# Two first loads without a cast on the hardware queues, and a new written-out order, in an attention and mixer kernel

## The chip, the cores and the metric

One core of one Trainium2 chip. The metric is the time of one launch on the device in microseconds (us). The kernel before has a median of 415.73 us in 3 runs (415.58 to 415.92). One execution was profiled; its trace gives every instruction and every transfer.

Engines: PE (TensorE, matrix products), DVE (VectorE), ACT (ScalarE), POOL (GpSimd) and SP (SyncE). POOL, SP and ACT issue transfers (DMA). Transfers that POOL issues can cast float32 to bfloat16 on the way; this kernel issues all its casting loads there. What SP and ACT issue is not cast.

## The reference: what is computed

Linformer attention, then one mixer block, all inputs float32. B = 8 batches, H = 8 heads, S = 1024 positions, D = 64.

```python
k_proj = np.einsum('ks,bhsd->bhkd', E, k)        # 64 rows in place of 1024
v_proj = np.einsum('ks,bhsd->bhkd', F, v)
scores = scale * np.matmul(q, k_proj.transpose(0, 1, 3, 2))
...
attn = attn / (np.sum(attn, axis=-1, keepdims=True) + 1e-09)
x = np.matmul(attn, v_proj)                      # heads side by side: (8, 1024, 512)
...
h = np.maximum(x.transpose(0, 2, 1) @ w_tok1, 0.0) @ w_tok2
u = x + h.transpose(0, 2, 1)
h2 = np.maximum(u @ w_ch1, 0.0) @ w_ch2
return u + h2
```

## The kernel before

**Work.** For each batch: kv_proj (L503) projects k and v with E and F, two heads at a time in batch 0; k_transpose (L564) and q_transpose_pe (L608) turn k and q on PE; scores (L630) multiplies them, and ACT takes the exponential; attend (L658) multiplies with v, where a column of ones gives the sum of each row; DVE takes its reciprocal into rdn (L686) and multiplies (L692) into x. The token mixing follows (L1050 and L1079 in batch 0, others later), then the channel mixing: up_set (L1163, matmuls in L1180) and down_block (L1254, matmuls in L1289), each as a Strassen-like scheme of seven products. Nearly all of PE's time goes to the channel mixing.

**Batch 0.** Everything stands still until its data are there. The heads come in pairs; the pair of heads 2 and 3 is worked first, then 4 and 5, 0 and 1, 6 and 7. A pair's k, v and q are three loads of 512 KB each in memory (256 KB once they are bfloat16). All come by POOL's queue: 12 loads for the attention of batch 0, then w_tok1 (two), w_tok2, w_ch1 (six), w_ch2 (four), with batch 1 between and behind them. E and F come as float32 on SP's and ACT's queues (L257, L258) into the tile o0, which only later holds outputs; PE turns them (L462) with an identity matrix that POOL makes (L450), and ACT and DVE copy them to EFT as bfloat16 (L465).

**What sets the order.** The function adds jobs to a Planner (L116): each has an engine, a time that the author gives it, what it reads and writes, and a function that issues the instructions. plan() (L158) does not choose: it decodes ORDER, a string with two characters for each job, and SPOTS, one digit for each use of a PSUM bank. The jobs are issued in that order, and each engine executes its own in the order issued. FILLS names the places in the order ahead of which PE gets a product of zeros (blank, L435) that nobody reads. So ORDER, SPOTS and FILLS are the schedule of all engines, POOL's loads included; the times in the jobs served whoever made the strings and do not reach the chip.

At the start PE executes four products of zeros (L446), two of bfloat16 and two of float32. HWK (L90) is 0: the lines at 260 and 379 that would load k and v uncast do nothing.

**Reciprocals.** rdn_t (L295) has two tiles; attention pair g writes tile g % 2, so the next but one pair writes over it.

Of the kernel before, what the change touches and what calls it, by code (L numbers as in the profile page):

```python
# [9 lines left out]
F32 = mybir.dt.float32  # L10
# [10 lines left out]
    "4w3o5A424x4y0l5B4e0j4h5p4b4f454j464i4k3r5C4z0m43475D5E4l444-0o4m503s4o4n3t4+4p5q525t514B5F4q5r4C495s"
    "530p544D3Z5y3u5w0q5H3bA15x4J3c3a6B5u5I554K5z4r4G4L5K5v4A4H9v5L9x6D484I5+6E0r6F564M6C5-6G6O4N6A606P6Q"
    "626H6I6L4O636561646Z6J674s666K4EA26a57684F6M6b696N4Q0n6f4P6U6g6R6W4R6S6h6Y4U4S6V6c6i6T6X5S4T6d6j6k6u"
    "6l6e5T6m6n6x6+6v5U6o4V6-6y6z716p5a6q4W5G705b725J746r7A73756s765M6t776wA35N7B5O585Q787C5R4t5X5P795Y7J"
    "7F7K7D7G7H7Q7EA57I5Z7L7R5dA759A85eA65VA95fAAA45W5c5h5g5i7V7S5l7TAD7Z7X4X5m5j7a7n5k5n7b7o7W7d5o9z7M7e"
    "7p9-7c7O7q7g7P7r7h7N7f7sAF7i7uAH7Y7lAG7t7m7v7jAJ837wAIANAK7x84ALAOAhAM7z7yAiAP877kAj857U7+88AQAb8986"
    "ARAS8AAcAdAk8BAWAlAm8L9yAZ8CAYAeAT8DAfAaAg8FAUAXAV8M8G8EENB3At7-Az8N8mAEA+8+8i8n8TA-EO8k8oAuAvABAn8H"
    "8U8pB4B5AC8-8q81B0Aq8r92Ao8J90Ap938QArAs8jB6AwB18tB2B795Ax8uB88R8l91Ay8s96B9948v8w9G978x8yBB9H988SBD"
    "999I8KBE9KBCBF8z8WBGEP8VEQ9L9ABABI9N9BBJBH9O9+8X9JBKBNA0BLBO8Y9QBM829MBPBRBSBV8I8aBWBQBTBk9R80BYBXBl"
    "8bBZBUBn9PBc8OBdBa9SBeBfBpBbBh8PBgBmBiER9CBj8ZBo9YEVES9TBr9ZEUBqET8eBs9aEW8f8c9UBu8d9g9W9E9hEYBtC1Bz"  # L30
    "9dEZC2B-9iBwC59VC3BxC69eC48gC89D8hEbC9Bv9bEdC0Ec9c9FEfEj9fCBEeEgEkElCC9jB+EmEhEi9kEn9XEpEr9lC7EoCFCA"
    "By9nCGEsEtCDEq9oCEEu9mCJCHEvEwExCI9r9pCKCXEyEz9qCLCYCME+CNCZEaE-F09sCaILCOCPF19tIMCbDACREXCcF2F4F3Cd"
    "CQ9uF5CeF6CpCfF7FBDCChCSFCDEF9CqDFFADSCiCgFDCrDICTFEDGDJF8FGCjFHFFDHFLDTFICxCkFMFJFPClDUCmFKDLDBDVFQ"
    "FNDDDMFTCVCyINFUFRFODKCnFWDWFXCuDXDNFYCvCzFaCwFVDZFbDQDaC+DRFiFcDODcFSDPFZFdFfFeIPFjFgDdCUFhFlIRDYIT"
    "DkDbISCsIQCWDlFkIUIOC-CoFmFnDeD0CtFoFpDoFqD2DpD1D3FxIXDmD4D6DnIWFzFsFrDrD5FtDqDsFuF-DtD7G0DfDuD8G1Dv"
    "DwF+G2DgG3E0FvG4E1DiDxFwIZE2DyG6IbD+E8G7DjE9IcDzIdGDEAIaE5FyGEG9DhIeGAE6IfD-IhIgGHIiGFIjGIG5GGIkG8IY"
    "GVInE7GKMKIoGBImEBGCGLIsIlECItIuIpGNIqIrIvGOE3IwEDGWE4IxI-GZJ0EEIyGaEFJ1EGIzI+EJEHGXJ5EIJ2GYGcJ3J4GJ"
# [12 lines left out]
    "PiRRPgRcOOPhRSOvRMRTRPRUOwUJRdRVPjRWPaRXUNRfUKRZRYOyULRaRhUMPlRgRbReUOPmPwRiPkRjPnPxRkOzPcPoOmO+PpRl"  # L50
    "RmPyO-PqRnOnRrRoQ2RtOxRvPrQ3RwRpP0Q4RqP1RxP2S7RyPsRzPuUPPbR+P-UQRuPvURS0RsQ0S8S1UUSBUVQ1S9SCS3UWSAQ5"
    "PdUTUXS4SEUYUZUSR-SDSFS2UaSGQ6UbUdS5Q7SJUePtUfUcQ9UgUhSPT3SHSKSQUoQASIUpS6STT2UrUqSUSRT6UsSSQBSWUlUt"
    "QCSXPzUmT7T4P+UnUiQ8TASZUjUkShSLT8UxUuT9QDUvSaUwSVUzQESYU-SiU+V0TBSbT5QFV1TCSNV2QGTDSjUyV4P3TETcScV5"
    "V3TFSpV6SqSdSOV9SfV7VASeTGTdVDSMTKV8THTeSrTIVHTJVBVISmVETLVFVCSnVKTgVLVMThTMSoVJTfVOVGTjTNVPVWTkTOVQ"
    "TiTPVRTlVTSsVNStVUVXTRVSTmTSSgVZVVTQTnVaTuTTToSuSkTpTWTqSwTXSxTYVdVYSySlTsSzTvVeTUSvVbVlTVVgVpVnS+Vf"
    "VqVcS-TwVmVtT0U0VuVoT1W1VhU1W2TaViVwVjVrVxU2W5VkWJW6VvWKTzVyT+WNT-V-W8W0VzU3WOW9W7VsU4WAV+WQTrWPTZWR"
    "WLWSW3WDU5W4X0TtWBWyWTTbWCXIWMWzWVW+WUTxWEX1TyWFU7U6U8WWX4W-U9UBWXWbUAWZX2XaX3UCX5WcXbUDXJX7WYXcWdWH"
    "X6XdWGXMX8WgXNX9WhXPXCXQXAXDXeWiWjXfWaXOXBXEXKXGWmXRXLWIWkXUWlWnXVXhWoWeXiXWXgWqXjWrXmWfXnXkXoXSWsXs"
    "XTWpWtXtXlXHUEXYWuXZXuXpWvXqXFX-XXX+WwXxWxXyXvY9XzXrY0XwY1Y4Y2Y3Y6Y5Y7YAYDY8YBYCYJYFYEYMYGYKYNYHYLYO"
    "YIYPYQ"  # L60
)
SPOTS = (
    "3024101126436327273643040127120236363170420436171063240217145624732113405063774765765024721257605205"
    "6726211311072323401724223063354705252601467407364317023117417326261333177136413604752570156153207422"
    "0717501237102275300221337643164504125123103737627351104724633607633666334154626574653573657273116524"
    "1713476526117451111000431363504562017414020567306256407306640427552552201753173152014723475602015723"
    "0720475332734202200176315612415716323744645200150524671"
)
FILLS = (21, 21, 21, 21, 21, 21, 21, 27, 27, 30, 36, 36, 36, 36, 49, 62, 62, 66, 66, 79, 79)
# [20 lines left out]
HWK = 0  # L90
# [97 lines left out]
def kernel(  # L188
# [54 lines left out]
    def tile_of(shape, dtype, name):  # L243
        return sb.tile(shape, dtype, tag=name, name=name)
# [15 lines left out]
    for i, queue in enumerate((nc.sync, nc.scalar)[:HWK]):  # L260
        queue.dma_start(out=kv32[i], in_=(k, v)[i][0, 0:2].rearrange("h (p si) d -> p h si d", p=P))
# [33 lines left out]
    rdn_t = [tile_of([P, NJ, 2, 2], F32, f"rdn{i}") for i in range(2)]  # L295
# [82 lines left out]
    lead = (1.95, 2.45, 3.2)[HWK]  # L378
    for i in range(HWK):
        pl.add("SPQ", 1.6 + 1.1 * HWK, 1.6 + 1.1 * HWK, lambda: None, writes=[("kv32", i)], prio=-1001)  # L380
        if i:
            act(
                1024, lambda: nc.scalar.copy(out=v_sb[:, 0:2], in_=kv32[1]),
                reads=[("kv32", i)], writes=[("v", 0), ("v", 1)], prio=-100,
            )
        else:
            dve(
                1024, lambda: nc.vector.tensor_copy(out=k_sb[:, 0:2], in_=kv32[0]),
                reads=[("kv32", i)], writes=[("k", 0), ("k", 1)], prio=-100,
            )  # L390
# [63 lines left out]
    opening.append(pl.add("POOL", 1.0, 3.2, identities, writes=["ident"], prio=-150))  # L454
    pl.opening = opening

    for n in range(2):
        b = Bank("S", full=False)

        def turn(n=n, b=b):  # L460
# [9 lines left out]
        pl.add("PE", 0.9, 0.9, turn, reads=["ident"], takes=[b], prio=-150).mms = NJ  # L470
# [1091 lines left out]
```

## Time and profile before

| what | value |
| --- | --- |
| median of 3 runs | 415.73 us |
| the profiled execution: its time | 415.69 us |
| the profiled execution: first to last instruction (span) | 413.9 us |
| granted TensorE clock | 0.999 |
| DVE, ACT, POOL busy | 86%, 54%, 16% of the span |
| casting loads on POOL's queue: share of 16 engines | 55.7% of the span |
| E and F: issue to landing | 3.2 and 3.8 us |
| PE waiting, all waits that the profile lists | 3.4 us, 2.3 of it for the first loads of q and for the first memset |

The time of a run is the span and what lies around it, 1.8 us here. A busy PE is one with any matmul under way; a row of the timeline lasts from the first start to the last end, and matmuls overlap, so the pace is read from the starts. In the answers on windows, the columns are the stretch and its length, busy us and count of instructions for PE, its weight loads (PEld), DVE, ACT and POOL, then the granted clock, the mean busy share of the DMA engines and the GB/s that were written. Of a casting load, the written bytes are half of the read ones.

### The profile page before, as it was taken

The numbers are of one execution on the slowest core, as the hardware profiler recorded it, in microseconds if no ns is written. First come the engines' busy times: TensorE is split into PE (matmuls) and PEld (weight loads), VectorE is DVE, ScalarE is ACT, GpSimd is POOL, SyncE is SP. The second block draws the span as 40 slices with busy tenths as digits, with TensorE's granted clock in tenths as the row PEclk, the third lists the DMA queues.
The fourth block names the chain that finished last, engine by engine and source line by source line (L and its number), as shares of the span: only waits on it lengthen the run. The fifth ranks groups of instructions, "written<-read, shape, count | busy, mean of one in ns | idle before, by whom it ended". The sixth has DMA issues, their size and how long they took to land.

```text
span 413.9 us, 9589 instructions
## 1 busy us (share of the span) xinstructions
PE 406.4 (98%) x3909; PEld 344.4 (83%) x3911; DVE 355.9 (86%) x773; ACT 221.9 (54%) x429; POOL 66.8 (16%) x105
## 2 busy tenths in 40 slices
PE   8899999999999999999999999999999999999996
PEld 4489888688888888979988899888988798998896
DVE  2289899779999999989979798898989899988686
ACT  1647884258635664574754646455644745445520
POOL 8544021021102120112001112012100001010010
PEclk9999999999999999999999999999999999999999
DMA  8999999997998897978966869873996212251115
GB/s 153 205 202 204 207 190 192 160 172 170 189 166 168 201 170 143 166 156 156 245 118 127 133 148 178 143 167 89 180 227 118 52 51 103 52 115 39 52 69 187
DMA packets 93755, 61.69 MB, mean 149 GB/s; under 512 B 59024, under 2 KB 89232, under 8 KB 93712
## 3 DMA queue, kind: packets, MB, share of 16 engines
q0 software_dynamic: 35088, 45.09, 55.7%
q1 hardware_dynamic: 58256, 15.47, 22.8%
q8 instruction: 30, 0.49, 0.5%
q10 hardware_dynamic: 368, 0.52, 0.3%
q14 instruction: 13, 0.11, 0.1%
HBM read 59.24 MB, written 16.78 MB: 184 GB/s over the span
## 4 chain that ended last, share of the span: by engine, by line
PE 92%; DMA 4%; DVE 2%; POOL 1%; issue 1%; POOLq 0%; DVEq 0%
PE psum L1289 36%; PE psum L1180 35%; PE psum L991 5%; PE psum L875 4%; PE psum L672 3%; PE psum L521 3%; DMA q_sb<-in_q_dram 3%; PE psum L637 2%; DMA v_sb<-in_v_dram 1%; PE psum L712 1%; PE psum L1060 1%; PE psum L736 1%; DVE u L1105 1%; PE psum L1092 1%; PE psum L618 1%
## 5 line engine op out<-in xcount | busy, mean ns | idle before, releaser
L1289 PEld LDWEIGHTS <-G 128*128 128x128 bf16 x1356 | 130.0, 98 | 18.3 <-issue 3.5
L1289 PE MATMUL psum<-wc_sb,G 128*128 128x256 bf16 (+1 forms) x780 | 101.5, 271 | 0.0
L1180 PEld LDWEIGHTS <-wc_sb 128*128 128x128 bf16 x768 | 73.9, 98 | 10.5 <-issue 2.1
L1202 ACT ACTIVATE G<-psum 128x512 bf16<-128x512 f32 x96 | 56.2, 601 | 44.8 <-PE psum L1180 44.3
L1289 PE MATMUL psum<-wT,G 128*128 128x256 bf16 x576 | 75.6, 273 | 0.1
L1216 DVE TENSOR_TENSOR G<-G 128x512 bf16<-128x512 bf16 (+1 forms) x140 | 69.4, 515 | 0.8
L1180 PEld LDWEIGHTS <-wT 128*128 128x128 bf16 x576 | 55.3, 98 | 7.3 <-issue 0.6
L1180 PE MATMUL psum<-S,wc_sb 128*128 128x256 bf16 x384 | 56.2, 273 | 0.0
L1180 PE MATMUL psum<-S,wT 128*128 128x256 bf16 x384 | 56.0, 273 | 0.1
L1180 PE MATMUL psum<-uT,wc_sb 128*128 128x256 bf16 x384 | 55.5, 273 | 0.0
L1326 POOL DMA_DIRECT2D out_dram<-o x30 | 16.4, 548 | 212.7 <-DVE o L1332 171.2
L692 DVE TENSOR_TENSOR x_sb<-psum,rdn 128x256 bf16<-128x256 f32 (+1 forms) x88 | 46.7, 540 | 1.8
L1332 DVE TENSOR_TENSOR o<-psum,u 128x512 f32<-128x512 f32 x59 | 39.9, 681 | 3.7 <-PE psum L1289 3.3
L1208 ACT COPY ub<-psum 128x512 f32<-128x512 f32 x48 | 28.1, 588 | 23.4 <-PE psum L1180 18.5
L652 ACT ACTIVATE a<-psum 128x512 bf16<-128x512 f32 x64 | 34.9, 603 | 8.5 <-PE psum L637 8.3
L1161 DVE CUSTOM_DVE_ANT_0 G<-psum,ub 128x512 bf16<-128x512 f32 x48 | 32.7, 683 | 6.9 <-PE psum L1180 6.6
L1223 ACT COPY psum<-psum 128x512 f32<-128x512 f32 x48 | 27.6, 579 | 18.6 <-PE psum L1180 13.0
L1161 DVE CUSTOM_DVE_ANT_0 G<-psum,ua 128x512 bf16<-128x512 f32 x48 | 32.6, 684 | 5.3 <-PE psum L1180 4.4
L1208 ACT COPY ua<-psum 128x512 f32<-128x512 f32 x48 | 28.3, 590 | 14.0 <-PE psum L1180 13.6
L1180 PE MATMUL psum<-uT,wT 128*128 128x256 bf16 x192 | 28.7, 273 | 0.0
L358 POOL DMA_DIRECT2D v_sb<-in_v_dram x18 | 13.3, 742 | 75.4 <-PE psum L1180 22.7
L672 PE MATMUL psum<-vb,a 128*128 128x130 bf16 x256 | 25.3, 220 | 0.0
(102 smaller groups left out, 499.4 us busy)
## 6 DMA issues: line engine op xcount, KB each, us to landing
out_dram<-o POOLq DMA_DIRECT2D x30, 512.0 KB, 3.8
k_sb<-in_k_dram POOLq DMA_DIRECT2D x14, 512.0 KB, 11.2
v_sb<-in_v_dram POOLq DMA_DIRECT2D x14, 512.0 KB, 7.3
q_sb<-in_q_dram POOLq DMA_DIRECT2D x14, 512.0 KB, 9.2
wc_sb<-in_moe_w_ch_dram POOLq DMA_DIRECT2D x6, 256.0 KB, 11.9
wc_sb<-in_moe_w_ch_dram POOLq DMA_DIRECT2D x4, 384.0 KB, 13.3
k_sb<-in_k_dram POOLq DMA_DIRECT2D x4, 256.0 KB, 7.9
q_sb<-in_q_dram POOLq DMA_DIRECT2D x4, 256.0 KB, 8.1
```

The costliest lines, as they stand in the source:

```text
L652: lambda g=g, half=half, bk=bk: nc.scalar.activation(out=a_t[g][:, half], in_=bank(bk), func=ACT.Exp, scale=scale),
L672: nc.tensor.matmul(view()[:, k, c].rearrange("p i d -> p (i d)"), a_t[g][:, c, at : at + P], vb[:, g].rearrange("k i d -> k (i d)"), start ...
L692: lambda: nc.vector.tensor_tensor(out=x_sb[:, rows, g * P : (g + 1) * P].rearrange("p (n c) (i d) -> p n c i d", c=2, i=2), in0=view()[:, ...
L991: nc.tensor.matmul(view(X_OF[n])[:, r, :], tok2_of(n, i, r), T[n] if n in T else h[B[n]], start=(n in (1, 7) and r == 0), stop=True, skip_ ...
L1161: nc.vector._custom_dve(TENSOR_ADD_SAT, out=out, in0=in0, in1=in1, s0=FMAX, s1=0.0)
L1180: nc.tensor.matmul(t[:, c, :], w1_of(n, dd, 2 * m + c), a_of(j, n, dd), start=(n in (1, 7) and c == 0 and dd == 0), stop=(c == 1 and dd == 1),
L1202: lambda: nc.scalar.activation(out=G[:, n, cs], in_=view(src), func=ACT.Relu),
L1208: 512, lambda: nc.scalar.copy(out=dst, in_=view("y")), writes=[(name, s % 2)],
L1216: 512 * len(both), lambda: f(out=G[:, n, c], in0=G[:, a, c], in1=G[:, b, c]), ps=False,
L1223: 512, lambda: nc.scalar.copy(out=view("y"), in_=view("x")), takes=[bk["y"]],
L1289: nc.tensor.matmul(to, G[:, G_OF[n], cc, t * P : (t + 1) * P], w2_of(n, cc)[:, cut], start=(n in opens and (t == 0 or alone) and cc == 0), ...
L1332: 512, lambda: nc.vector.tensor_add(out=dst, in0=view(src), in1=u_of(sh, dh)),
```

## The change

- k and v of heads 2 and 3 in batch 0, the first pair that is worked, are loaded as float32, each as one transfer: k on ACT's queue behind F, v on SP's queue behind E, into the tiles o1 and o2. Four new jobs cast them into k_sb and v_sb, one head on DVE and one on ACT for each. The two loads are gone from POOL's list.
- The planner's times change: 4.5 us for E and F, 6.3 and 7.7 us for these k and v, 1.4 in place of 3.2 for the identities.
- One of the two float32 products of zeros at the start is gone.
- rdn has eight places, one for each of the four pairs of two batches in a row.
- ORDER, SPOTS and FILLS are new throughout. FILLS still has 21 entries; five stand ahead of the EF transposes.
- Of POOL's order at the start: before, k of heads 2 and 3, the identities, then q and v of heads 2 and 3, q, k and v of 4 and 5, k, v and q of 0 and 1, k, q and v of 6 and 7. Now q of 4 and 5, q of 2 and 3, v of 4 and 5, the identities, then k of 4 and 5, k, v and q of 0 and 1, k, q and v of 6 and 7. Later, k and v of batch 1 (heads 0 to 3) stand ahead of w_ch2 instead of in the middle of it, and q of batch 1 ahead of the last piece of w_ch2.

```diff
-FILLS = (21, 21, 21, 21, 21, 21, 21, 27, 27, 30, 36, 36, 36, 36, 49, 62, 62, 66, 66, 79, 79)
+FILLS = (11, 11, 11, 11, 11, 23, 23, 23, 23, 23, 23, 30, 37, 37, 37, 37, 37, 40, 82, 93, 117)
...
-    ("k", 0, 2), ("v", 0, 2), ("q", 0, 2), ("k", 2, 2), ("v", 2, 2), ("q", 2, 2),
+    ("k", 0, 2), ("v", 0, 2), ("q", 0, 2), ("q", 2, 2),
...
-    for i, queue in enumerate((nc.sync, nc.scalar)[:HWK]):
-        queue.dma_start(out=kv32[i], in_=(k, v)[i][0, 0:2].rearrange("h (p si) d -> p h si d", p=P))
+    for to, src, queue in zip(kv32, (k, v), (nc.scalar, nc.sync)):
+        queue.dma_start(out=to, in_=src[0, 2:4].rearrange("h (p si) d -> p h si d", p=P))
...
-    rdn_t = [tile_of([P, NJ, 2, 2], F32, f"rdn{i}") for i in range(2)]
+    rdn_t = tile_of([P, 2 * HP, NJ, 2, 2], F32, "rdn")
...
+    lead = 0.0
+    pl.add("SPQ", 4.5, 4.5, lambda: None, writes=["EF"], prio=-1003)
+    for i, (name, to) in enumerate((("k", k_sb), ("v", v_sb))):
+        pl.add("SPQ", 6.3 + 1.4 * i, 6.3 + 1.4 * i, lambda: None, writes=[("kv32", i)], prio=-1002 + i)
+        for h in range(2):
+            (act if h else dve)(
+                512,
+                lambda i=i, h=h, to=to: (nc.scalar.copy if h else nc.vector.tensor_copy)(
+                    out=to[:, 2 + h], in_=kv32[i][:, h]
+                ),
+                reads=[("kv32", i)], writes=[(name, 2 + h)], prio=-100 + i,
+            )
...
-    opening = [warm(zero), warm(zero), warm32(), warm32()]
+    opening = [warm(zero), warm(zero), warm32()]
...
+    attended = iter(range(2 * B * HP))
...
+        at = next(attended) // 2 % (2 * HP)
...
-            rdn = rdn_t[g % 2][:, 2 * half + jn[0] : 2 * half + jn[0] + n]
+            rdn = rdn_t[:, at, 2 * half + jn[0] : 2 * half + jn[0] + n]
```

More of the change, by code (lines that the diff above doesn't have):

```diff
@@ L21 @@
[L21 to L25, printed above, removed]
@@ new lines @@
+    "1m0J1b1c1p1U1e1q1f0w1V1r1W0L0y1y0x1s1v1z0-1+11100M1t1Y1-1Z121u2022210K0+0z132423141w1x2A0O15282B1619"
+    "1C1725180N291A2C27261B1F2E1G1D1E2D2W1H0P2b2R2X2S2L2F2c3G2M2G2I2O2H2d2Y2N2Z2J2T2K2U2P2e2Q2V2g2h2a2i2f"
+    "2-3F2j302p2k2l2q0Q2x2m2t2r2y0T332s2u2n2z2o37340S2v2+3P382w350c3B3Q3H0d39363L313R3N323C3z0R3S3h0e3A4g"
+    "3M0g3i3T3J0h3n0i3U3D0k3l0l3W3E3m3j0m3X3V0f3k3I3o3O3+0j433Y3Z3p3-0n3a3q3b4h414c3K403c3r3t4e424i4f3s3u"
+    "4k4j444d3d5t453f465E5v3v4l4y494z474A5w4n5x48504o4+5F4m5u4q4p51524-0s5I4r3x5G4B4s4D5y0t535z4F4t549z5+"
@@ new lines @@
+    "5J9-4G0o560p4H5L555-600q4NA50u5H584u5M9+4O613w4E5O4P4K573y5P4L4C0r6H4M626J3g6I3e594Q6E636K4w6M4R6F6L"
+    "6N0v666S4I656G4S646V6T696O6W6B6U6A6X6P67A64U6Q5A685B6d6D6C4J6e6R6j6f4V6k6l4v6Y4T6m6Z5W4W6a4Y6n6b6o4X"
+    "6s6p6c6g5X6h6q6r4Z6i5Y6t6u6-756y70725e717376746v5K775f6w5N787E6z6x6+5Q797A7B5g5R7F5S5U7C7G5C5VA75b4a"
+    "7D5T5c5D7H7L7I7N7M7J7U7OA97K7V7P5d7WAA4x7QAD5hAB7R5iAEA85Z5j5a5l5k5m7ZAH5p5n7d4b7a7r7b7e5qAC7s7h5r7f"
+    "7iA17t5s7g7S7X7u5o7k7c7v7T7lAJ7w7jAL7yAK7m7x7zA3AO87AM7+7pAN7nAPAQ887Y817q7oARAl8B827-8CASAUAT8980Am"
@@ new lines @@
+    "AVAfAWAo8A8EAn8DAg8FAhAaApAq8G8PAbA0AeAXAi8JAYAdAZ8HAjAkAcB18Q8KAI8IAxB2B4B38RESB78qAy8m92B5ER8rB68X"
+    "B88oAF8sB9AzAr8uAG8t8LBAAsAu938n8YBB8vAvBC96At948p978x8N95Aw8w838yA+99BD989A9K858+8z8U8-A-B08V9LBF9C"
+    "9BBH9DBE9OBI90BGBJ8W9EBKETBL91BM9F8aBN869P8bBO8ZBRBP8cBS9RBQA29M9SBTBV8M9N9QBW8OBZBo84BaBb8eBXBUBcA4"
+    "9U8fBd9VBYBeBp9TBg8SBhBr9WBiBj8TBfBkBlBqBtBmEVBsBn9G8d9cEW9XEYBv9dEX8g8iEaBwEU9e8h8jEZBx9YBy9k9I9l8k"
+    "C59aC1B+C69hC3B-C9Ed9mC7CA9i9ZC8BuCC9HEfCDBz9fEgC4Eh9g9JEjEn9jCFEiEkEoEpCG9nElEmEq9b9oErC2EtEv9pCBEs"
@@ new lines @@
+    "CJCE9rCKC0EwExCHEuCNCI9sCO9qEyCLEzE+E-CM9vF0F1Cb9tCQCcF29w9uCRF3F4CP8l9xCdEcCTCSCeCfDEIQF8CgF5F9CVEe"
+    "F6FACtEbF7CiDWCWIPCjFFFBCUDIFGFDClDJChFECmCuFCFHCkDKFICXFJFKDGCnFLDMCvCoFPDNFMC-DLCpDHFNDXDFD0FQCrFO"
+    "FTDYCZISFRD1DaDPFSDbCYDOFXFUDdCsFYCyFVDZFaDQCzFbDeFcC+FmDSFnCqFeDgDTFdD2DhFfFZDRFpFoFhFWFrFgCwFiD3Ca"
+    "FjDUFkCxFqFlITD4D5FsDAIUDVIVFtDoFuIWIYD6IRDpFvDcFwDsFxFyDtDqDfD7IXDrDiD8DvF-DBD9DjG39yFzDuG4DCE4DwG1"
+    "G5DDDkDyG6IbDxE5DzDmG7IaE6G0IdG8DlD+IhG2ECIfD-GAIeE0EDE2GBE3IlIgGHImInG9GIE9GCIiEEGDEAIjGEIkGLEBF+Io"
@@ L61 @@
+    "U7TvWHWSTfWFTxT-WGWIU8WQX1X2WUU9WTWVX4VwWWUBX5WXU0X8UAX6X9WJUCWYX3WZX7UFWaUGWbUDXBWdXAUEWeXeWLWfXfUH"
+    "WgXCUIXgXDWhXMWMXiXNWKXGWkXHWlWcXjXkWmXQXEWqXFXlXRWrXmXSXnXTWsXoXUXOXVWnXIXqWoXrXWWpXYXXWuXZXPWvXpXa"
+    "XhWiWwWjXcWxXKXwWtXxXsXtWyXbXyXuWzY3W+X-XvW-Y0XJY2Y4XzXLY1YDX+Y5Y6Y8Y7YAYBY9XdYCYHYFYNYEYGYIYJYQYKYO"
+    "YLYRYPYSYMYTYU"
 )
 SPOTS = (
[L63 to L64 removed]
@@ L377 @@
     w2t = moe_w_tok2.rearrange("(tc p) s -> p tc s", p=P)
[L378 to L389, printed above, removed]
+    lead = 0.0
[9 more added lines that the diff above has]
+                reads=[("kv32", i)], writes=[(name, 2 + h)], prio=-100 + i,
             )
@@ L452, in identities @@
         make_identity(nc, ident32)
-    opening.append(pl.add("POOL", 1.0, 3.2, identities, writes=["ident"], prio=-150))
+    opening.append(pl.add("POOL", 1.0, 1.4, identities, writes=["ident"], prio=-150))
     pl.opening = opening
@@ L468, in take @@
             )
-        pl.add("PE", 0.9, 0.9, turn, reads=["ident"], takes=[b], prio=-150).mms = NJ
+        pl.add("PE", 0.9, 0.9, turn, reads=["ident", "EF"], takes=[b], prio=-150).mms = NJ
         (dve if n else act)(512, take, writes=[("EFT", n)], uses=[b], prio=-150)
@@ L670, in mm @@
                     for c in range(2):
-                        at = (2 * half + jj) * P
+                        s0 = (2 * half + jj) * P
                         nc.tensor.matmul(
-                            view()[:, k, c].rearrange("p i d -> p (i d)"), a_t[g][:, c, at : at + P],
+                            view()[:, k, c].rearrange("p i d -> p (i d)"), a_t[g][:, c, s0 : s0 + P],
                             vb[:, g].rearrange("k i d -> k (i d)"), start=True, stop=True,
                         )
-            keys = [("rdn", g % 2, 2 * half + jj) for jj in jn]
+            keys = [("rdn", at, 2 * half + jj) for jj in jn]
             xs = [("x", 2 * g + i, half) for i in range(2)]
```

70 lines of the change are left out of this document (26 added, 44 removed).

## The prediction, made before the result was known

> **What bounds the kernel now.** I read the page first, then the waits of TensorE, its busy time by stretch, and the end of the opening as chain and timeline. The page's first part has TensorE (PE) busy almost throughout; the windows (columns: us, busy time and count of each engine, granted clock, DMA share, GB/s written) show where the rest is.
>
> ```profile
> PE 406.4 (98%) x3909; PEld 344.4 (83%) x3911; DVE 355.9 (86%) x773; ACT 221.9 (54%) x429; POOL 66.8 (16%) x105
> ```
> ```profile
> 25.00:45.00 20.00, 19.94 (x257) 18.52 (x257) 18.91 (x50) 13.36 (x27) 7.56 (x10) 1.00 1.32 202
> 45.00:100.00 55.00, 54.90 (x532) 43.95 (x532) 47.54 (x123) 34.61 (x68) 7.37 (x11) 1.00 1.08 191
> 100.00:200.00 100.00, 100.00 (x956) 86.22 (x954) 94.64 (x200) 56.64 (x111) 16.55 (x24) 1.00 0.93 163
> ```
> From 25 us on PE has 0.16 us of idle time up to 100 us and then none; the two stretches after that, up to 409.8, are full too. PE's work is the same in both kernels (the orders hold the same jobs, and 21 filler matmuls each), so the end can move only with the moment from which PE stays busy with real work, or by new holes later. Before 25 us the loads set that moment. Casting loads count 256 KB written for 512 KB read, so a full rate reads as about 204:
>
> ```profile
> 2.50:3.50 1.00, 1.00 (x3) 0.22 (x2) 0.00 (x0) 0.13 (x1) 0.93 (x4) 1.00 0.75 295
> 3.50:4.00 0.50, 0.50 (x3) 0.41 (x2) 0.00 (x0) 0.00 (x0) 0.50 (x2) 1.00 0.87 279
> 4.00:4.50 0.50, 0.50 (x2) 0.19 (x1) 0.00 (x0) 0.00 (x0) 0.50 (x1) 1.00 0.89 113
> 4.50:5.00 0.50, 0.50 (x2) 0.23 (x1) 0.00 (x0) 0.00 (x0) 0.50 (x2) 1.00 1.09 170
> 5.00:6.50 1.50, 1.50 (x6) 0.94 (x5) 0.00 (x0) 0.00 (x0) 1.50 (x3) 1.00 1.23 198
> 6.50:8.00 1.50, 0.79 (x8) 0.60 (x7) 0.69 (x1) 0.59 (x1) 1.50 (x3) 1.00 1.10 169
> 8.00:10.00 2.00, 2.00 (x16) 0.99 (x15) 0.69 (x1) 0.00 (x0) 1.58 (x3) 1.00 0.93 149
> 10.00:19.00 9.00, 7.97 (x95) 4.02 (x95) 2.08 (x9) 5.61 (x15) 4.75 (x7) 1.00 1.24 204
> ```
> The chain of waits (start, us, what) and PE's timeline tell which landings PE stands at:
>
> ```profile
> 3.87 6.17 DMA v_sb<-in_v_dram
> 10.34 11.12 DMA q_sb<-in_q_dram
> ```
> ```profile
> 19.02 0.63 PE L521 MATMUL psum<-k_sb,EFT_sb 128*64 128x128 bf16 x8 [0.17 <-DMA k_sb<-in_k_dram]
> 21.50 0.62 PE L618 MATMUL psum<-ident,q_sb 128*128 128x128 bf16 x8 [0.45 <-DMA q_sb<-in_q_dram]
> 24.13 0.55 PE L1060 MATMUL psum<-x_sb,wt_sb 128*128 128x128 bf16 x7 [0.16 <-DVE x_sb L692]
> ```
> The third load (v of heads 2 and 3) lands at 3.87 + 6.17 = 10.04, the tenth (k of 6 and 7) at about 19.0, the eleventh (q of 6 and 7) at 10.34 + 11.12 = 21.46. From third to tenth one load takes (19.0 - 10.04) / 7 = 1.28 us: the queue is full there. The eleventh takes 2.5. Dense work starts at 24.13, 2.67 behind that q.
>
> **The change, part by part.** *Loads.* k and v of heads 2 and 3 leave the POOL queue and go uncast behind F and E, 512 KB each, as many bytes read as before. So q of heads 6 and 7 still has ten loads ahead or beside it: it comes earlier only by DMA time that now lies idle. From the rows, against 204: 91 x 0.5 + 34 x 0.5 + 6 x 1.5 + 35 x 1.5 + 55 x 2 = 234 KB from 4 to 10 us, 234 / 204 = 1.15 us. From 2.5 to 4 us, against 408 uncast: (113 + 129 x 0.5) KB / 408 = 0.43 us. Gain s of the loads: at least 0 (no idle time is filled); at most 19.0 less a gapless row of ten, 4.3 + 10 x 1.28 = 17.1, that is 1.9, plus 0.43, or 2.3. I take **1.2**: the uncast megabyte is queued by about 2 us (its issues follow E's and F's, 0.57 us each), needs no POOL instruction, and lies in wait through most of the gap.
>
> *When the first pair lands.* E and F land 3.2 and 3.8 us after issue at 0.74 and 0.76, so at 3.9 and 4.6. If k and v run alone after that: 4.6 + 2 x 1.28 = 7.2. If they take turns with three casting loads: 4.6 + 5 x 1.28 = 11.0. The planner's entries say 6.3 and 7.7; I take these, being nearer the first. Then casts (0.59 on ACT, 0.69 on DVE, by the L465 rows, from PSUM), and the first projection at 8.5 instead of 9.9 to 10.1. At the far end it starts at 11.8, and the next barrier, k and v of heads 4 and 5 (13.85 now, by the 1.28 row), still ends later. So this head start is worth nothing by itself: the later landings pace PE.
>
> *Casts.* Two of 0.7 us on DVE and two of 0.6 on ACT, in stretches where DVE is busy 1.38 of 5 us and ACT 0.59 of 5. Behind them in line stand the two EFT copies; if k were 1.5 us late, EFT and the first projection would be too, still before that barrier. Cost 0, at worst that same head start.
>
> *POOL.* Three loads go ahead of the identities (1.05 us, from 2.10 to 3.15), which end at 1.28 + 3 x 0.72 + 1.05 = 4.5, when F lands: hidden. The fourth casting load is issued at 4.5, needed at 4.6 + 5 x 1.28 = 11. The opening: one float32 filler (1.71) less, five bfloat16 ones (0.43 each before the clock rises) more, +0.4 us on the EF transposes, ahead of copies that wait for k: 0.
>
> *Reciprocals.* Eight places against two take away only ordering; writer and reader are both DVE, which runs in order. 0 by itself.
>
> *Order.* Up to the first token-1 product (L1060), the new order has done two more units of pair 2 (four matmuls, 4 x 57 ns = 0.23 us by the pace of L672 at 21.96) but has kT of pair 3 behind qT on ACT (0.27) and a filler (0.22) there. Before has another stop of 0.28 us after 24.13. Net between -0.3 and +0.5; I take a gain of **0.2**, the middle being 0.1 and the extra units certain. Further on I looked for a load that comes too late: batch 1's first k and v now stand before w_ch2, and one w_ch2 piece goes behind q. A w_ch2 piece lands at 37.6 before (issue 25.09, 12.5 to landing); with four pieces of 1.9 us and three loads of 2.6 from 35.7 on, the last lands at 51.1 - 1.2 = 49.9. Its first reader on DVE stands at 36.4 us of PE work; the first L1289 stands at 35.6 in the old order and starts at 52.1, so this is 52.1 + 0.8 - 1.4 = 51.5. It holds, with 1.6 us to spare.
>
> **Sum:** 415.69 (profiled execution, span 413.9 and 1.8 around it; median of the runs 415.73) - 1.2 - 0.2 = **414.3**.
>
> A rule that speaks against it: the Trainium skill, "SBUF — State Buffer", section "SBUF: two separate sides", says that a float32 SBUF-to-SBUF copy on DVE locks GpSimd out, so that it cannot write descriptors and the DMA engines starve. Both new DVE casts are of that kind. No such copy stands in the trace between 4 and 10 us (the copies there read PSUM), so it does not explain today's gap; it could make a new one, and by it the time would be that of the first rival below.
>
> **Rivals.**
> 1. *Starvation comes back.* The gap of 4 to 10 us coincides with POOL issuing back to back (DMA_DIRECT2D rows from 3.15 to 9.58), and POOL still does in the new kernel, with the new casts beside it. Then s is 0 to 0.3, and 415.69 - 0.1 - 0.2 = 415.4. For it: 149 GB/s while loads were queued. Against: the uncast loads pass by POOL. Chance 0.19.
> 2. *The new order stops PE further on.* DVE is at 18.91 of 20 us from 25 to 45; a job placed too late there costs its own length, about 0.7 (an L1332), and two undo the gain: 415.0 to 415.7. Against: with DVE as full as this, PE shows 0.16 us of idle time in those 75 us. Chance 0.10.
> 3. *Slower: the hardware queues run slowly.* E and F moved 512 KB between about 2.1 us, where the windows first show bytes, and 4.2 (F's landing less the 0.3 us after a last byte): 2.1 us, against 1.28 for a casting load of as many bytes. At that pace k and v hold the engines 2 x 0.82 = 1.64 us longer, ahead of all that follows: 415.69 + 1.64 - 0.2 = 417.1. It decides from 1.28 + 0.7 = 2.0 us each. Against: the slow part of E and F is their start (295 and 279 are counted with the ramp). Chance 0.08.
>
> **How the numbers follow.** Forecast 0.63. The range takes both ends of s (2.3 + 0.2 gives 413.2; 0 and a small loss gives 415.9); left out are rival 3 and some 0.08 around the ends. A measurement here can tell 0.2%, 0.8 us, from no change. Faster by more: the forecast's 0.63 and a part of rival 2, 0.67; within: rival 1 and most of rival 2, with a rest of the forecast, 0.22; slower: rival 3 and a worse order, 0.11.
>
> **What would show it.** Right: GB/s without the dip to 149 from 4 to 10 us, q of heads 6 and 7 landing near 20.3, the first L1060 at 22.5 to 23.2, and PE full from there. Wrong: that q at 21.2 or later (rival 1); idle PE after 25 us (rival 2); k and v landing after 9 us with the next loads behind them (rival 3).

## The result, and the profile after

The kernel after is slower: 418.56 us median of 6 executions (416.83 to 418.74) against 415.68 us for the kernel before, measured beside it, a ratio of 1.0060 (95% interval 1.0046 to 1.0074). The forecast was 414.3 us (413.2 to 415.9). The six executions form two groups: two at 416.83 and 417.04 us with a granted clock of 1.0, four at 418.45 to 418.74 us with 0.994 to 0.996. The profiled one is the shortest: 416.83 us, span 415.0, clock 1.0. So the trace explains 1.1 us, and 1.7 us more stand only in the four others; the experiments had to show these. The ratios in this text are the record's estimates and not quotients of the medians.

First the trace, by the same windows as before (us, busy time and count of PE, PEld, DVE, ACT and POOL, granted clock, DMA share, GB/s written).

```profile
4.00:4.50 0.50, 0.50 (x3) 0.22 (x2) 0.00 (x0) 0.00 (x0) 0.43 (x3) 1.00 0.80 307
4.50:5.00 0.50, 0.50 (x3) 0.19 (x2) 0.00 (x0) 0.00 (x0) 0.50 (x2) 1.00 1.07 369
5.00:6.50 1.50, 1.50 (x8) 1.07 (x6) 0.00 (x0) 0.00 (x0) 1.50 (x3) 1.00 0.94 231
6.50:8.00 1.50, 1.50 (x11) 0.92 (x10) 0.98 (x2) 0.98 (x2) 1.50 (x3) 1.00 1.12 287
8.00:10.00 2.00, 0.57 (x3) 0.15 (x2) 0.73 (x2) 0.65 (x2) 0.95 (x2) 1.00 1.20 233
...
100.00:200.00 100.00, 99.30 (x946) 85.29 (x944) 94.10 (x196) 54.97 (x107) 17.09 (x25) 1.00 0.96 161
```

GB/s rises between 4 and 10 us to 231 to 369 from 113 to 198, but that does not show the dip filled: GB/s counts what is written, and a float32 load writes twice what a casting load writes for the same bytes read. The queues from 4 to 10 us, before's casting queue first, then after's three (packets, MB written, share of the engines):

```profile
q0 software_dynamic: 1007, 0.98, 105.4%
```
```profile
q0 software_dynamic: 589, 0.57, 58.4%
q1 hardware_dynamic: 272, 0.52, 26.3%
q10 hardware_dynamic: 252, 0.48, 22.3%
```

With the casting loads counted twice, before read 1.97 MB there and after 2.15. At the forecast's full rate, 408 GB/s read, the 0.18 MB more are 0.45 us, where it had most of 1.15 us filled. And PE is busy only 0.57 us between 8 and 10 us, and it has 0.7 us of holes between 100 and 200 us, where before had none. PE's timeline (start, us, line, operation, what ended the idle time ahead of it) shows both places:

```profile
8.32 0.24 PE L519 MATMUL psum<-k_sb,EFT_sb 128*64 128x128 bf16 x1
10.14 0.22 PE L519 MATMUL psum<-v_sb,EFT_sb 128*64 128x128 bf16 x1 [1.58 <-ACT v_sb L384]
```
```profile
20.78 0.61 PE L616 MATMUL psum<-ident,q_sb 128*128 128x128 bf16 x8
...
23.55 0.67 PE L1062 MATMUL psum<-x_sb,wt_sb 128*128 128x128 bf16 x9
```
```profile
134.40 0.82 PE L1291 MATMUL psum<-wc_sb,G 128*128 128x256 bf16 x6
135.76 0.62 PE L635 MATMUL psum<-qT,kT 64*64 64x512 bf16 x8 [0.54 <-DMA qT<-q_sb]
```

The uncast k landed at 7.00 and v at 9.45, not at 6.3 and 7.7; PE waited 1.58 us for v's cast. The q of heads 6 and 7 landed at 19.40 (21.46 before), so its transposes at 20.78 show no wait; the first token-1 product came at 23.55 (24.13). At 135.8 PE waits for a transpose of q.

To say where time goes in the body, I compare executions at equal PE work: matmul columns are added up along the trace, and the moments at which two kernels reach the same sum are subtracted. The reference is the execution of the first experiment below (before's order, span 414.7), because before's own trace lacks some 0.45 us of matmul records between 70 and 100 us. Negative is ahead of the reference.

| execution (clock 1.0) | at 34 us | 44 | 101 | 142 | 273 | 404 |
| --- | --- | --- | --- | --- | --- | --- |
| after | -1.07 | -0.62 | -0.73 | -0.14 | +0.29 | +0.49 |
| e9 (before's order from 100 us) | -0.93 | -0.49 | -0.60 | -0.69 | -0.68 | -0.18 |
| e13 (before's order from 26 us) | -1.13 | -1.11 | -1.20 | -1.19 | -1.18 | -0.69 |
| e12 (before, new order from 100 us) | -0.47 | -0.45 | -0.45 | -0.13 | +0.30 | +0.32 |
| e15 (before, eight places) | -1.05 | -1.02 | -1.04 | -1.03 | -0.52 | -0.52 |
| e14 (before, eight small DMAs) | -0.22 | -0.21 | -0.23 | -0.22 | -0.21 | +0.12 |

Read the first row: the opening's 1.07 us are there at 34 us, 0.45 go by 44 us, 0.6 near 136 us, 0.6 in small pieces later; at 404 us after is half a microsecond behind. The reference is itself one execution, and one of the best behind 100 us: between 101 and 404 us the twelve traces with before's order there change by -0.1 to +0.5 against it (mean 0.25), the seven with the new order by +0.7 to +1.2 (mean 0.83). So the new order's own price there is some 0.6 us on average, not 1.2. The waits of after between 34 and 45 us name the first of these, Strassen sums of weights that DVE makes too late (us in total, times, longest):

```profile
PEld L1182 <- DVE wT L474: 0.5, 2, 0.3
```

**The end.** Behind the last landing SP walks a list of waits on DMA semaphores, in the order of their numbers but for the last. These are SP's semaphore records in the two traces (us from the span's start):

```
before: last landing 412.99; S[118] 413.01, S[111] 413.07; end of span 413.91
after:  last landing 413.27; S[109] 413.29, S[111] 413.36, S[112] 413.86, S[115] 413.94,
        S[116] 414.00, S[117] 414.07, S[118] 414.13, S[113] 414.20; end of span 415.04
```

Before's last output has the last but one semaphore of the list. In after it has an early one, so six more waits of 0.065 us come behind the landing, and a pause of SP of 0.5 us with them, which in before (411.39 to 411.86) lay under the wait for landings: 1.77 us from landing to end in place of 0.92.

### The profile page after: what moved, and what is told of

Read it like the earlier page. It is cut to its first block, busy times and chain, and to the rows that moved or that the text cites. A ratio compares the mean times of both kernels' runs of the same rounds, so it can differ in the third digit from the quotient of the medians.

```text
span 415.0 us, 9598 instructions
## 1 busy us (share of the span) xinstructions
PE 406.0 (98%) x3909; PEld 343.8 (83%) x3909; DVE 358.5 (86%) x775; ACT 222.2 (54%) x431; POOL 65.4 (16%) x103
## 3 DMA queue, kind: packets, MB, share of 16 engines
q10 hardware_dynamic: 640, 1.05, 0.8%
## 4 chain that ended last, share of the span: by engine, by line
PE 86%; DVE 6%; DMA 4%; issue 1%; ACT 1%; SPq 0%; DVEq 0%
PE psum L1182 33%; PE psum L1291 32%; PE psum L877 4%; PE psum L993 4%; PE psum L674 3%; PE psum L519 3%; DMA qT<-q_sb 2%; PE psum L635 2%; DMA o<-in_v_dram 2%; DVE x_sb L694 1%; PE psum L738 1%; PE psum L1062 1%; PE psum L1094 1%; PE psum L714 1%; DVE o L1334 1%
## 5 line engine op out<-in xcount | busy, mean ns | idle before, releaser
L1291 PEld LDWEIGHTS <-G 128*128 128x128 bf16 x1356 | 129.8, 98 | 18.3 <-issue 3.3
L1182 PE MATMUL psum<-S,wT 128*128 128x256 bf16 x384 | 56.9, 273 | 0.1
```

The lines of the kernel that those rows point to most:

```text
L1182: nc.tensor.matmul(t[:, c, :], w1_of(n, dd, 2 * m + c), a_of(j, n, dd), start=(n in (1, 7) and c == 0 and dd == 0), stop=(c == 1 and dd == 1),
L1291: nc.tensor.matmul(to, G[:, G_OF[n], cc, t * P : (t + 1) * P], w2_of(n, cc)[:, cut], start=(n in opens and (t == 0 or alone) and cc == 0), ...
```

## The experiments

Three theories: **A**, two more hardware DMAs turn the semaphores, and the end grows; **B**, the new order loses in the body what the opening gains; **C**, formed after the first four runs: the wait for the casts lets TensorE's clock fall. Ratios are to the kernel before, measured beside it, with 95% intervals.

**e1, before with two small DMAs.**
```diff
+    scr = tile_of([4, 4 * 8], F32, "scr")
+    for i in range(2):
+        nc.sync.dma_start(out=scr[:, 4 * i : 4 * i + 4], in_=E[0:4, 4 * i : 4 * i + 4])
```


> The kernel before with two more DMAs of 64 bytes on SyncE's hardware queue at its start, into a tile that nothing reads; nothing else differs. Theory A (the waits that SP walks at the very end stand in the order of semaphore numbers, and two more hardware DMAs turn the last output's semaphore from the last of that list to an early one, so that what is left of the list runs behind the last landing): last landing as before (near 413.0), end of the span 0.8 us later than before's, about 414.7, and the time 416.5 against 415.7. Rival (the longer end belongs to the new order or to the fp32 loads): no change, span 413.9, time 415.7.

Measured: 416.32 against 415.25, ratio 1.0026 (1.0017 to 1.0036). Theory A holds in direction. In the trace the last landing is at 413.45 on S[109], seven waits follow where before has one, and the end is 1.28 us behind the landing, not 0.92: 0.36 of the 0.85; SP's pause fell ahead of the landing this time. The landing itself took 2.52 us from issue, 0.5 more than before's.

**e14, before with eight.** The same lines with `range(8)`.

> The kernel before with eight small hardware DMAs at its start, so that the semaphores of all others turn once round to where they were. Theory A (what cost 1.07 us with two of them is the place in the list at the end): within 0.3 us of before, ratio 1.000. Rival D (such DMAs cost by themselves, at the start): 1 us or more over before, ratio 1.0025 or more, and the kernels with six more must be read as that much better.

Measured: 415.41 against 415.39, ratio 0.9998 (0.9988 to 1.0008). Eight turn the semaphores round once, and the loss is gone: the small DMAs cost nothing by themselves. In the trace the last landing is on S[117], last but one of the list again, and the end is 0.92 us behind it. So the position in the list is what e1 pays for behind its landing, 0.36; what makes 1.07 of it in the median stays open.

**e2, after with six.** The same lines with `range(6)`.

> The kernel after with six more DMAs of 64 bytes on SyncE's hardware queue at its start, so that the hardware DMAs are eight more than before's in all. Theory A (the place of the last output's semaphore in the list of waits at the end): the end is again as before's, under 0.1 us of SP's waits behind the last landing; span about 414.2 where the clock is at 1.0 against 415.0, the time 0.8 under that of the kernel after at the same clock. Rival: the end stays as it is, 1.1 us between last landing and end of the span. Second question, the granted clock: if it was the chip that the kernel after was measured on, all runs here are at 1.0; if the kernel itself draws the clock down, some are at 0.995 and 1.7 us longer.

Measured: 417.16, ratio 1.0045 (1.0029 to 1.0062). The time alone says nothing on the end, since two executions have clock 1.0 (416.25, 416.30) and four 0.995 (417.0 to 418.2). The trace does: the last landing is on S[117], and the end stands 0.93 us behind it, against 1.76 to 1.77 in after, e3 and e5. Six small DMAs take the 0.85 away, as theory A says. The kernel before, measured beside it on the same chip, has 23 executions, all at 0.999 or 1.0. So the clock follows the kernel.

**e3, one transpose moved.**
```diff
 925 first transpose of q, third batch
+926 second transpose of q
 ... 753 transpose of u, 932 transpose of k
-926 second transpose of q
```


> The kernel after with one step moved: the second transpose of q of the third batch stands on SP directly behind the first one, ahead of the transposes of u and of k, as in the kernel before. Theory B (the new order's own stops give the opening's gain back, and this transpose, landed at 135.7, is the dearest with 0.7): the stop at 135.8 is gone and the time is 0.5 to 0.7 lower than the kernel after's at the same clock, about 416.2. Rival (what the transpose waits for is only the first of several causes that end at the same place; the next is as late): less than 0.2 lower, with PE waiting for another tile within 10 us.

Measured: 417.5, ratio 1.0056 (1.0037 to 1.0074); again three executions at 1.0 (416.18 to 417.10) and three at 0.994 to 0.996 (417.9 to 419.07). Undecided by time.

**e4, before's order from 100 us.** Steps 560 and on in before's relative order.

> The kernel after up to the 560th step of its order (about 100 us), with the loads, casts and eight places as they are, and from there the steps in the relative order of the kernel before, with PSUM banks as before's; nothing else. Theory B (the loads' gain of 1.1 us at 33 us is real and what is lost behind it belongs to the order): about 0.8 us of gain still there when the last output lands (412.2 against 413.0), the longer end of 0.85 remains: time about 415.7 at clock 1.0. Rival (the body loses the gain whatever the order, since other work was covering it): last landing at 413.0 or later, time 416.6 or more.

Measured: 416.18, ratio 1.0025 (1.0013 to 1.0038), with six of eleven executions at 0.994 or 0.995 (415.95 to 417.87) and the others at 415.06 to 416.18. The page of this execution, and of those of e2 and e3, has an 8 in the slice from 10 to 21 us:

```profile
PEclk9899999999999999999999999999999999999999
```

PE's gap ahead of the first projection was 2.18 us in e2, 2.69 in e3 and 2.40 in e4, and 1.58 in after's profiled execution, which kept its clock. That gave theory C.

**e5, after again.** No edit.

> The kernel after, unchanged, beside the other three of this call on one chip. Theory C (TensorE waits 1.6 to 2.7 us for the casts of k and v, by how late these two land; where the wait is over some 2 us the granted clock goes to a half for some 4 us soon after, which adds 1.5 us): two groups of runs, clock 1.0 near 416.5 and clock 0.994 to 0.996 some 1.5 us longer. Rival (the chip of the first measurement): all runs at 1.0.

**e6, eight more fillers.**
```diff
-FILLS = (11, 11, 11, 11, 11, 23, 23, 23, 23, 23, 23, 30, 37, ...
+FILLS = (11, 11, 11, 11, 11, 23, 23, 23, 23, 23, 23, 23, 23, 23, 23, 23, 23, 23, 23, 30, 37, ...
```


> The kernel after with eight more fillers (the matmuls on zeros, 0.2 us each) ahead of the first projection of k and v, so that TensorE has 14 there and not 6, and waits for the casts about 1 us and not 1.6 to 2.7; nothing else. Theory C: every run at clock 0.998 or more, none of the longer group, median near 416.5, some 1 us below the unchanged kernel after of this call. Rival (the dip comes from the denser work behind the wait, or from the chip): as many runs at 0.995 as without them.

Measured: e5 418.28 (417.42 to 418.33), ratio 1.0056 (1.0039 to 1.0073), four of five executions at 0.994 to 0.996 and one, 418.32, at 0.999, which theory C leaves unexplained; e6 416.50, ratio 1.0020 (1.0009 to 1.0030), every one of its 11 executions at 0.998 or more. PE's wait in e5, then windows of e5 and of e6; the column ahead of the last two is the clock:

```profile
PE psum L519 <- ACT v_sb L384: 2.3, 1, 2.3
```
```profile
8.00:10.00 2.00, 0.00 (x0) 0.11 (x1) 0.43 (x1) 0.62 (x1) 0.99 (x2) 1.00 1.22 232
10.00:11.00 1.00, 0.97 (x23) 0.87 (x23) 0.31 (x2) 0.00 (x0) 0.40 (x1) 0.97 1.24 204
11.00:12.00 1.00, 0.93 (x8) 0.34 (x6) 0.71 (x3) 0.00 (x0) 0.43 (x2) 0.50 1.24 206
12.00:13.00 1.00, 1.00 (x10) 0.88 (x9) 0.02 (x1) 0.88 (x2) 0.44 (x1) 0.50 1.24 205
13.00:14.00 1.00, 1.00 (x3) 0.30 (x2) 0.67 (x1) 0.30 (x1) 0.54 (x1) 0.50 1.25 205
14.00:15.00 1.00, 1.00 (x7) 0.26 (x5) 0.00 (x0) 0.00 (x0) 0.51 (x1) 0.82 1.23 203
```
```profile
8.00:10.00 2.00, 2.00 (x10) 0.79 (x9) 0.74 (x2) 0.84 (x2) 0.91 (x2) 1.00 1.20 234
10.00:11.00 1.00, 0.88 (x21) 0.82 (x22) 0.23 (x1) 0.07 (x1) 0.41 (x2) 1.00 1.24 206
11.00:12.00 1.00, 0.61 (x9) 0.28 (x6) 0.79 (x4) 0.00 (x0) 0.44 (x2) 1.00 1.24 205
12.00:13.00 1.00, 1.00 (x12) 0.70 (x12) 0.39 (x1) 0.84 (x2) 0.46 (x1) 1.00 1.24 204
13.00:14.00 1.00, 1.00 (x8) 0.29 (x6) 0.30 (x1) 0.34 (x1) 0.54 (x1) 1.00 1.25 205
14.00:15.00 1.00, 1.00 (x18) 0.58 (x18) 0.00 (x0) 0.97 (x2) 0.50 (x1) 1.00 1.24 206
```

In e5 PE does nothing from 8 to 10 us, and a microsecond after it starts again its clock is at half. With fillers it is busy all of that time and keeps the clock. Eight matmuls on zeros take 1.8 us off the median. Of the 0.96 us that e6 is still over before, its trace has 0.85 at the end, which stands 1.77 us behind the landing as in after.

**e8, the gap alone, in before.**
```diff
-FILLS = (21, 21, 21, 21, 21, 21, 21, 27, 27, 30, ...
+FILLS = (27, 27, 30, ...
 ... 78 first projection
+85, 86 transposes of q and their copy (were ahead of 78)
```


> The kernel before without the seven fillers ahead of its first projection, and with the first transposes of q behind that projection, so that TensorE has nothing from 7.1 us until k and v have landed at 9.9; loads, casts and the rest as before. Theory C (the wait alone does it): clock near 0.995, half of full speed for about 4 us from 11 to 15 us, and a time 1.5 us or more above before's. Rival (the dip belongs to the fp32 loads, their casts or the new order): the clock stays at 1.0, and the time within 0.5 us of before's, since before's opening waits for loads anyway.

Measured: 416.79 against 415.54, ratio 1.0031 (1.0017 to 1.0046). Eight of eleven executions have a clock of 0.992 to 0.996, three 0.999 or 1.0 (415.51 to 416.30). The gap was 2.32 us (7.09 to 9.41):

```profile
9.41 0.26 PE L521 MATMUL psum<-v_sb,EFT_sb 128*64 128x128 bf16 x1 [2.32 <-DMA v_sb<-in_v_dram]
```
```profile
8.00:10.00 2.00, 0.59 (x12) 0.59 (x13) 0.00 (x0) 0.00 (x0) 1.95 (x4) 0.75 1.19 183
10.00:11.00 1.00, 1.00 (x15) 0.83 (x12) 0.00 (x0) 0.00 (x0) 0.47 (x2) 0.50 1.19 190
11.00:12.00 1.00, 1.00 (x6) 0.33 (x4) 0.58 (x1) 0.00 (x0) 0.62 (x1) 0.50 1.23 203
12.00:13.00 1.00, 0.58 (x3) 0.11 (x2) 0.94 (x5) 0.08 (x1) 0.56 (x1) 0.80 1.25 208
```

Theory C holds without any part of the change: the wait is enough to lower the clock.

**e7, everything mended, first attempt.** Before's order from step 180 (33 us), the eight fillers, six small DMAs.

> The kernel after up to the 180th step of its order (about 33 us), from there the steps in the order of the kernel before; eight more fillers ahead of the first projection; six more hardware DMAs of 64 bytes at the start. Theories A, B and C together: the opening's gain of 1.1 us stays to the end, no dip of the clock, the end of SP's waits as in before: 1.1 us under the kernel before of this call (ratio 0.9973). Rival (the gain is lost in the body whatever the order): a ratio of 1.000 or more.

Measured: 420.13, ratio 1.0101 (1.0083 to 1.0120): a miss, by the seam between the two orders. The piece of w_ch2 that before's order reads there stood last of the four in POOL's line and landed at 47.6; PE waited 3.0 us from 46.6, long enough for a fall of the clock there (an 8 in the slice from 42 to 52 us):

```profile
DVE wT L477 <- DMA wc_sb<-in_moe_w_ch_dram: 3.6, 1, 3.6
PEld L1185 <- DVE wT L477: 3.3, 1, 3.3
PE psum L1185 <- DVE wT L477: 3.0, 1, 3.0
```

**e9, mended from 100 us, and e10, the same with the long end.** The kernel of e4 with the eight fillers; e9 with six small DMAs, e10 without.

> The kernel after up to the 560th step of its order (about 100 us), from there the steps in the relative order of the kernel before; with the eight more fillers and with six more hardware DMAs of 64 bytes. Theories A, B and C: at 100 us the kernel after stands 0.75 us ahead of before (against a run of before's order whose records are complete), before's order keeps that distance, the clock stays at 1.0 and the end is as in before: 0.75 us under before, ratio 0.998. Rival (before's order gives the gain back too): ratio 1.000 or more.

> The same without the six further DMAs, so that the last output's semaphore stands third in the list that SP walks at the end. Theory A: 0.4 us more than the kernel with them (six waits of 0.065 us), 0.85 where SP's one pause of 0.48 us falls behind the last landing too. Rival: the same time as with them.

Measured: e9 415.70 against 415.37, ratio 1.0008 (0.9998 to 1.0018); e10 415.88, ratio 1.0015 (1.0006 to 1.0024). Before's order does keep the distance (table: -0.60 at 101 us, -0.68 at 273), but a stop of 0.4 us at 320 us follows, and the median does not show the 0.75 that I expected. That stop is none of the change's: PE waits 0.16 to 0.27 us for the same sums of DVE in e7, e13, e14 and e17 too, and e14 is before with small DMAs alone. The end's price by these two medians is 0.2, and their intervals overlap; in the traces it is 0.39 (0.92 us from landing to end in e9, 1.31 in e10).

**e11, fillers and the transpose early.**

> The kernel after with the eight more fillers (clock at 1.0, 0.96 us over before in its own call) and with the third batch's second transpose of q ahead of those of u and k. Theory B: the stop of 0.7 us at 136 us is gone, 0.5 us less than the kernel with the fillers alone: 0.45 over before, ratio 1.001. Rival (another stop takes its place): 0.9 over before, ratio 1.002.

Measured: 416.65 against 415.37, ratio 1.0032 (1.0020 to 1.0045), 5 executions: no gain in time over e6's 1.0020. In the trace the stop is gone (no wait of PE is listed between 100 and 200 us), and between 101 and 142 us only 0.07 is lost where after loses 0.59. But e6, which leaves the transpose where it was, lists no wait there either and loses 0.02. The stop comes and goes between executions of the new order (0.5 us of waiting in after, 0.3 in e2, 0.2 in e5), so one trace does not show that the move removed it. And this execution was 0.8 us behind after already at 34 us, which asks what varies in the opening.

**e12, the new order on before.** Before with eight places (the new order's dependencies need them), steps from 554 (100 us) in after's order.

> The kernel before (casting loads on POOL, its own opening) with eight places for the reciprocals, up to the 554th step of its order (about 100 us), from there the steps in the order of the kernel after. Theory B (the order alone costs it): about 1.2 us lost between 120 and 410 us, clock at 1.0, the end as in before: 1.2 us over before, ratio 1.003. Rival (the fp32 loads or what they shift cost it): within 0.3 us of before.

Measured: 415.84 against 415.37, ratio 1.0010 (0.9999 to 1.0022); in the trace 0.77 us are lost between 101 and 404 us, with the stop near 136 us of 0.3. Theory B's sign, at two thirds of its size in the trace; the interval of the time just includes no change.

**e15, the eight places alone.** The lines on rdn of the change in the kernel before.

> The kernel before with eight places for the reciprocals in place of two, its order, loads and banks unchanged. All theories: no change, ratio 1.000 within 0.1%. Rival D: a part of the loss, ratio 1.001 or more.

Measured: 415.36 against 415.39, ratio 0.9996 (0.9985 to 1.0007): nothing, as forecast.

**e13, the new opening only; e17, the same again; e16, the copies first.** After up to step 120 (26 us), then before's order, eight fillers, six small DMAs. e16 adds this:
```diff
+35, 37 copies of E and F out of PSUM, ACT and DVE
 3, 2   casts of k, ACT and DVE
-35, 37
 6, 5   casts of v
```


> The kernel after up to the 120th step of its order (about 26 us, where TensorE has become dense), from there the steps in the relative order of the kernel before; eight more fillers ahead of the first projection; six more hardware DMAs of 64 bytes. Theory B in its full form (what the new order loses, 0.4 us between 35 and 44 us and the rest behind 120 us, is all that eats the gain; the opening's gain was 0.3 to 1.1 us, by run): 0.3 to 1.1 us under before, ratio 0.9975 to 0.9993. Rival D (something else of the new opening costs as much as it gains, the extra DMAs or the eight places): ratio 1.000 or more.

> The kernel of the new opening only (e13), with the two copies of E and F out of PSUM placed ahead of the casts of k on ScalarE and VectorE; nothing else. Theory E (in the runs in which k lands last of the two, near 9 us, the copies stand behind k's casts though E and F landed at 4.3, and v's casts behind both, so that the first projection starts at 10.1 to 10.5 and not at 9.9): the late group of runs goes, some 0.4 us less in those, the median 0.2 to 0.4 us under e13's in this call. Rival (the spread of runs has another cause, such as where the fetch of instructions falls): the same median as e13.

> The kernel of the new opening only (e13), unchanged, beside the other on the same chip: by its first measurement 0.1 to 0.4 us over before (ratio 1.000). Theory E: the same again, and slower than the one with the copies first. Rival: the same as that one.

Measured: e13 415.86 against 415.39, ratio 1.0003 (0.9992 to 1.0014); e17 415.43 against 415.36, ratio 1.0007 (0.9998 to 1.0016); e16 415.00, ratio 0.9991 (0.9980 to 1.0001). The two executions profiled for e13 and e17 are among the shortest of theirs, 414.96 and 414.89; the others reach 416.4. With the copies first, the eleven executions lie between 414.78 and 415.28. The move of the copies does it, so the order of ACT and DVE is the cause. Which executions it hurts is argued: those in which k lands last. Here is ACT in e11, where k landed at 9.27, behind v (6.12):

```profile
9.30 0.62 ACT L384 CAST k_sb<-o 128x512 bf16<-128x512 f32 x1 [5.76 <-DMA o<-in_k_dram]
9.82 0.58 ACT L463 CAST EFT_sb<-psum 128x512 bf16<-128x512 f32 x1
10.30 0.62 ACT L384 CAST v_sb<-o 128x512 bf16<-128x512 f32 x1
```

The copy of E and F and v's cast, whose data were there, stand behind k's cast, and the first projection starts at 10.45. In the traces of after and its relatives k landed last in five (e3, e4, e7, e10, e11; 8.80 to 9.27) and v in the others. Of those that kept their clock up to 34 us, the three with k last stand 0.2 to 0.7 us ahead of the reference there, the others 0.8 to 1.1. No slow execution of e13 or e17 left a trace. e16 is the best kernel found, 0.36 us under before by the medians, with an interval that just includes no change.

## Why the prediction was wrong

- **Loads: the right way, and half the size.** I forecast that q near 20.3; it landed at 19.3 to 20.5 in all executions of the new opening. But in five executions of before's opening it landed at 21.46, 21.36, 20.93, 20.52 and 19.79. The one I worked from was the latest. A fetch of instructions (16 KB on one DMA engine, about 1 us) falls between 18.7 and 19.5 us there; in the first three this q lands 2.3 to 2.5 us behind the load ahead of it, in the last two 1.3. In 17 of all 19 traces one load that lands within 2.6 us behind the start of that fetch takes 2.0 to 2.6 us; in after it is the next one, v (21.68), so part of q's gain of 2 us there is luck. That the fetch delays it is not shown by an experiment. The tenth load, k of heads 6 and 7, where it kept its 1.3 us, landed at 17.9 to 18.3 in seven traces of the new opening and at 18.3 to 19.3 (mean 18.8) in six of before's loads: 0.6. At 34 us, before's opening stands at 0.02, 0, -0.22, -0.47 and -1.05 against the reference, a mean of -0.34; the new one, at clock 1.0, at -1.14 to -0.28 in eight executions, mean -0.90. The gain is near 0.56, not 1.2, with the two groups spread over 1.1 and 0.9 us. The term s was too large by half because I took most of the idle DMA time as filled; the queues show 0.45 of 1.15 us from 4 to 10 us. And "GB/s without the dip" was no sign of it, since k and v uncast had to raise the written bytes.
- **"I take these, being nearer the first", and "this head start is worth nothing by itself": the step that failed.** The later of k and v landed at 8.8 to 9.5, and I priced lateness at nothing up to 11.0, because a later barrier hides it. k and v shared the engines with casting loads, nearer the case of 11.0 that I set aside. The barrier hides the work, not the clock: in every trace in which PE idled 2.2 us or more there, the clock fell to half. That costs 1.2 us in the traces of e5 and e6 at 34 us (with 1.8 between their medians; the rest I can't place). For the same reason "one float32 filler less ... 0" was wrong: fillers are the cover of that wait, and I never named what they cover.
- **Order: "Further on I looked for a load that comes too late ... It holds".** True of that load (no wait for it in after), and too narrow: DVE's sums are late at 35 to 41 us (0.45, in every execution with the new order there, and in one of those with before's order, e8, with 0.34), SP's second transpose of q stands behind those of u and k (landed at 135.7, a stop of 0 to 0.6 by execution), and the rest goes in pieces. Against the mean of before's order the price behind 100 us is 0.6, so by the traces -0.2 should have been about +1.0; the median of e12 shows 0.5 of it. This was rival 2, given 0.10; its mechanism on DVE was right, and SP's queue was not in it.
- **"1.8 around it":** the time around the span held, but the end inside the span did not. Two DMAs more cost 0.4 to 0.85 us there; I did not look at what ends the span.
- **Reciprocals** 0, POOL 0: held. Rivals 1 and 3 did not come: from 4 to 10 us more was read than before, and the loads behind k and v keep 1.28 us each. The copy rule of the Trainium skill, "SBUF — State Buffer", section "SBUF: two separate sides", has no effect here that the windows show: the DMA share is 1.12 and 1.20 in the two rows with the casts.

By the medians, the 2.74 us of e5 over before are: the clock 1.78 (e5 to e6; 1.2 in their traces), the order behind 100 us and the end together about 0.6 (e6's 0.96 to e9's 0.33, measured on two chips). The traces say more for these two, 0.6 and 0.85; the difference is open. The copies standing behind k's casts cost 0.43 in the median (e17 to e16). The 0.45 at 35 to 41 us is shown by traces only: the medians of e9 and e13 do not separate it.

## What to carry to other kernels

Where an engine's clock depends on its activity, a wait that is off the critical path can still have a price once it is long enough: give every fillable wait its length, its spread from run to run and what covers it. Work that is ready should not stand behind a cast that waits for a transfer, above all where two transfers may land in either order. An order made from one trace's delays inherits that trace's luck; compare openings over several traces, and read the queue of every engine, SP's too, behind the point where the change ends.

## What the runs showed of the hardware

- Gaps of PE of 2.18, 2.30, 2.32, 2.40 and 2.69 us near 8 us, and 3.02 at 46.6, brought the clock to a half in the profiled executions; gaps of 1.58 us and less did not. The half lasted 3.4 us each time: in e5's rows (1 - 0.97) / 0.5 + 3 + (1 - 0.82) / 0.5 = 3.42. The Trainium skill, "TensorE: Matmul & The Clock Gate", section "HAM oscillation — how this bites in real kernels", asks for idle gaps above some 3.4 us. The length of the half agrees with that figure; as a limit on the gap it is too generous here, since 2.18 us was enough.
- The falls stand on a grid. In the clock records of the traces each fall inside the work came a whole number of steps of 3.41 us behind the first rise to full clock (at 3.9 to 6.7 us): one step in e8, two in e2, e3, e4 and e5, thirteen in e7. So the half began 0.1 to 2.0 us behind the gap's end in after's relatives, and 0.4 ahead of it in e8. What counts by these traces is PE's idle time within one step. Here are a step of after with 1.30 us of idle time and no fall behind it, then steps of e2 and e8 with 1.85 and 2.12 and a fall:

```profile
6.46:9.87 3.41, 2.11 (x13) 1.06 (x11) 1.68 (x3) 1.50 (x3) 2.36 (x4) 1.00 1.16 258
```
```profile
8.75:12.17 3.42, 1.57 (x28) 1.23 (x29) 1.55 (x5) 0.62 (x1) 1.62 (x3) 1.00 1.24 205
```
```profile
5.57:8.98 3.41, 1.29 (x10) 0.97 (x9) 0.69 (x1) 0.59 (x1) 3.41 (x6) 1.00 1.17 185
```

No step of the 19 traces with up to 1.61 us of idle time had a fall, and one at the very end of e5 had none with 1.93, so an estimate of the limit is 1.6 to 2.0 us in a step. After's gap of 1.58 us had 1.3 in one step and 0.3 in the next. The grid began at 6.5 us in after's trace and at 4.1 in e5's, the same kernel; so where a gap lies on it can count beside its length.

- Two transfers of 512 KB, issued within 0.04 us of each other on two hardware queues, landed in either order: k first at 5.9 to 7.2 us with v at 9.2 to 9.5, or v first at 6.1 to 8.1 with k at 8.8 to 9.3.
